# Gated linear attention with a mixture of experts: half of the values by POOL's queue, the output gate as a load of its own, and another order of SP's list of transfers

## The chip, the cores and the metric

The kernel runs on one core of a Trainium2 chip. The metric is the device time of one execution in microseconds (us); several executions of the same kernel are timed and their median is given. The core has five engines that follow lists of instructions of their own: TensorE (PE), VectorE (DVE), ScalarE (ACT), GpSimd (POOL) and SyncE (SP). SP does no arithmetic here, it issues transfers. POOL does arithmetic and issues transfers too, on a queue of its own. All transfers are carried out by the core's 16 DMA engines.

## The reference

Two stages follow each other. The first is a recurrent attention with gates, for 4 batches x 8 heads, 768 time steps and 40 values a head. The second takes its output as 3072 rows of 320 values, picks the best two of 8 experts for each row from noisy logits, and adds up the two experts' two-layer networks (320 to 1024 to 320).

```python
for t in range(S):
    m_new = max(f[t] + m, i[t])
    C = exp(f[t] + m - m_new) * C + exp(i[t] - m_new) * v[t] k[t]^T
    n = exp(f[t] + m - m_new) * n + exp(i[t] - m_new) * k[t]
    y[t] = sigmoid(o_gate[t]) * (C q[t]) / max(|n . q[t]|, 1)
x = y as (3072, 320)
logits = x @ w_gate + log1p(exp(x @ w_noise)) * noise
top2, weights = best two logits of a row, softmax over these two
out[row] += weight * (relu(x[row] @ w1[e]) @ w2[e])    for both experts e of the row
```

## The kernel before

**Attention.** The recurrence is computed in blocks of 64 time steps. A *unit* is one such block of two batches with all their heads, 128 rows of x; there are 24 units (`NU`), in two runs of 12 (`NCH`). The two batches of a unit are its two *halves*: half 0 sits in partitions 0 to 63, half 1 in partitions 64 to 127. For a unit u:

- `load_unit(u, what)` (L164) issues its loads on SP: q and k for the scores (tile `qk`, two transfers, L169), and the tile `vk`, two transfers of 64 rows x 968 values (L173 for half 0, L174 for half 1). One such row holds the 328 values with their ones, 320 of k, and 320 of the output gate. Each tile has four slots, so unit u uses slot u % 4.
- `e_part` (TensorE, L323, and ACT's exponential, L326) makes the decay weights `w` from the gates; `s_part` (L343, L346) the scores from `qk`; `k_part` (DVE, L354) weighs k; `p_part` (DVE, L360) multiplies scores and weights to `p`; `c_part` (TensorE L374, ACT L377) carries the state on into the next unit's slot of `vk`; `o_part` (TensorE, L383) makes the outputs from `vk` and `p`.
- `sig_part` (ACT, L332) turns the output gate (`SG`, a part of the `vk` tile) into its sigmoid in place, in three steps; `f_part` (DVE L388 to L394, POOL L395) divides and multiplies by it: the result `xr` is the unit's 128 rows of x.
- `keep_rows(u)` (L397) stores `xr` in DRAM: on POOL's queue for the first 12 units, on SP's afterwards. `t_part` (TensorE, L406) transposes `xr`, and from that the two gates of the experts, the choice of two, and the ranks of rows within their experts are computed, spread over the later steps.

**The main loop** (L821 on) runs over i with three units in hand: in turn i it computes the output of unit i, the scores of unit i + 2 and the weights of unit i + 2, and loads unit i + 3. Units 0 to 3 are loaded before and at the loop's start. What one turn puts into SP's list is, in this order: the stores of gate weights that are waiting in a list `sent` (L825; they write `wts`, the two weights of each row of earlier units, which POOL computes at L592), the loads of unit i + 3, the store of x of unit i − 1, in every second turn three small moves of attention gates (`gate_move`, L234 to L240: `le` and `re` out of `hl`; POOL issues them in turns below 13, SP later), and pieces of the first expert's W1 (L132), of constants or of noise. SP works through its list in order: an instruction whose inputs or whose slot aren't ready holds all that stand behind it. The same holds for POOL, whose list has, besides `xr`, the stores and the gate moves, a part of W1's split into two numbers (`w1l`, L142), `wts` and memsets.

**Experts.** From about 132 us on TensorE multiplies the gathered rows (`xg`, gathered by POOL at L779, rows transposed at L809) with each expert's W1 and W2, in two-number precision (L1003, L1032 to L1034). The outputs are scattered by POOL (L1055).

The order on TensorE, DVE and ACT is written out by hand by these calls, and `fill` and `SHARE` decide how much of the choice of experts goes into a turn.

Of the kernel before, what the change touches and what calls it, by code (L numbers as in the profile page):

```python
# [18 lines left out]
NE, F, DM = 8, 1024, 320  # L19
L = 64  # L20
TA = 4
NCH = S // L
NU = 2 * NCH
# [29 lines left out]
VW = 968  # L53
# [10 lines left out]
@with_exitstack  # L64
def build(ctx, tc, qk, vk, fi, noise, wgn, w1, w2, cst, ce, out):
    nc = tc.nc
    V, A, P, T, SP = nc.vector, nc.scalar, nc.gpsimd, nc.tensor, nc.sync
# [49 lines left out]
    SG = [t[:, 0, 648:VW] for t in VKS]  # L117
# [45 lines left out]

    def load_unit(u, what="kv"):  # L164
        pr, c = divmod(u, NCH)
        if "k" in what:
            r = 0
            for a, step, n in DIMS:
                SP.dma_start(QK[u % 4][a:128:step], qk[pr, c, r:r + n])  # L169
                r += n  # L170
        if "v" in what:
            flat = VKS[u % 4].rearrange("p x c -> p (x c)")
            SP.dma_start(flat[0:64, 0:VW], vk[pr, c, 0])  # L173
            SP.dma_start(flat[64:128, 648:648 + VW], vk[pr, c, 1])  # L174

# [24 lines left out]
    SP.dma_start(fit[:, :, 256:512], fi[:, :, 256:512])  # L200
    load_unit(0, "v")

# [68 lines left out]
    load_unit(1, "k")  # L271
    load_unit(1, "v")
    blank(2, P)
# [10 lines left out]
    for i in range(2, 4):  # L284
        keys(i)
    load_unit(2, "v")
    load_unit(3, "k")
# [109 lines left out]
    def keep_rows(u):  # L397
        (P if u < XV - 1 else SP).dma_start(XD[128 * u:128 * u + 128, 0:DM], XR[u])
# [274 lines left out]
    sent = []  # L673
# [45 lines left out]
    gate_move(2)  # L719
    load_unit(3, "v")  # L720
    SP.dma_start(fit[:, :, 512:], fi[:, :, 512:])
# [98 lines left out]
    i = 0  # L820
    while i < NU - LEAD:  # L821
        unit[0] = i
        spent[0] = 0.0
        while sent:
            SP.dma_start(*sent.pop())  # L825
        if 1 <= i and i + 3 < NU:
            load_unit(i + 3)
        if i:
            keep_rows(i - 1)
        if i % 2 == 0 and i and i // 2 + 2 < 2 * GB:  # L830
            gate_move(i // 2 + 2, (P, P) if i < XV else (SP, SP))
# [7 lines left out]
        if i == 5:  # L839
            SP.dma_start(nzt, noise)  # L840
        if not begun and done[0] >= E0U[0]:
            decode(0, E0S[1] // 128, 128 * E0U[0] > FIT)
            begun = 1
# [60 lines left out]
    u = NU - 2  # L904
# [19 lines left out]
    u = NU - 1  # L924
# [395 lines left out]
def layout(i):  # L1320
    import numpy as np
    z = lambda *s: np.zeros(s, np.float32)
    qk = z(2, NCH, 2, D, 2, H, L)
# [4 lines left out]
    qk = np.concatenate([qk[:, :, :, d].reshape(2, NCH, -1, 2, H, L) for d in (slice(0, DA), slice(DA, D))], 2)  # L1328
    vk = z(2, NCH, 2, L, VW)
    a = i["v"].reshape(2, 2, H, NCH, L, D).transpose(0, 3, 1, 4, 2, 5)  # L1330
    v = np.ones(a.shape[:-1] + (D + 1,), np.float32)
    v[..., :D] = a
    k, og = [i[n].reshape(2, 2, H, NCH, L, D).transpose(0, 3, 1, 4, 2, 5).reshape(2, NCH, 2, L, DM) for n in ("k", "o_gate")]
    for p in range(2):
        vk[:, :, p, :, 320 * p:320 * p + 328] = v.reshape(2, NCH, 2, L, 328)[:, :, p]
        vk[:, :, p, :, 320 * p + 328:320 * p + 648] = k[:, :, p]
        vk[:, :, p, :, 648 * (1 - p):648 * (1 - p) + 320] = og[:, :, p]
    fi = np.stack([i["f_gate"].reshape(2, 1, 16, S), i["i_gate"].reshape(2, 1, 16, S)], 3)
    fi = np.ascontiguousarray(np.broadcast_to(fi, (2, 2, 16, 2, S))).reshape(64, 2, S)
    nz = np.ascontiguousarray(i["moe_noise"].reshape(2, 2, NCH, L, NE).transpose(1, 3, 0, 2, 4)).reshape(128, NU, NE)  # L1340
# [5 lines left out]
    c, e = consts()  # L1346
    return dict(qk=qk, vk=vk, fi=fi, noise=nz, wgn=wgn, w1=i["moe_w1"], w2=i["moe_w2"], cst=c, ce=e)

# [19 lines left out]
```

## Time and profile before

| | us |
|---|---|
| median of 3 runs | 527.76 |
| lowest, highest | 525.27, 527.85 |
| the profiled execution | 528.23 |
| its span (first to last instruction) | 526.4 |
| TensorE busy | 504.1 |
| DVE, ACT, POOL busy | 343.1, 249.9, 215.7 |

The mean granted clock of TensorE is 0.993 of the full clock in the profiled execution.

A page of the profile has the busy time of each engine, a picture of the span in 40 slices, the DMA queues, a chain of work that ended last, and the costliest groups of instructions. Finer views answer questions: the instructions of one engine in order of time in a stretch (start, duration, engine, line, operation, tiles, count; in brackets the idle time just ahead of it and what ended this), the waits of SP's queue, the chain of waits in order of time, and a table of engines over stretches. Equal instructions in a row are merged in a line with their count, so the times of neighbouring lines of TensorE overlap. A line of the kernel is named L with its number. "SPq" is SP's list of transfers; its times are those of the issue, not of the transfer. Numbers of buffers are left out of names in these views.

### The profile page before, as it was taken

The page shows a single profiled execution, that of the slowest core. Times are in us where ns is not written, and L with a number is a line of the kernel's source. Part 1 is how long each engine was busy: PE and PEld are TensorE (multiplying, and loading weights), DVE is VectorE, ACT ScalarE, POOL GpSimd, SP SyncE. Part 2 cuts the span into 40 slices and gives each one's busy share as a digit, 9 for nine tenths or more (in the row PEclk, how much of TensorE's full clock was granted, in tenths as well). Part 3 has the DMA queues.
Part 4 walks back from the last instruction along what each step waited for, and adds up shares of the span by engine and source line. Part 5 has one row for each costly group of instructions (what it writes and reads, how often), then busy time and mean ns, then how long its engine had stood idle before and what let it go on. Part 6 is the DMA issues. An engine that isn't in the chain of part 4 may idle for free.

```text
span 526.4 us, 13193 instructions
## 1 busy us (share of the span) xinstructions
PE 504.1 (96%) x5052; PEld 473.3 (90%) x5053; DVE 343.1 (65%) x963; ACT 249.9 (47%) x607; POOL 215.7 (41%) x270
## 2 busy tenths in 40 slices
PE   9899998998999899999999999999999999999994
PEld 4778887987988788999999999999999999999994
DVE  8986979999887377763765485367447447645410
ACT  8877777888623145441543353154325415514300
POOL 6355455164012746145515623460553245042033
PEclk9998999999999999999999999999999999999998
DMA  5799797779767527069329515931762493272033
GB/s 155 191 258 246 212 228 199 191 217 252 262 197 243 96 40 207 17 124 256 84 55 269 103 37 105 265 91 37 213 141 63 97 263 86 55 175 25 2 36 44
DMA packets 49749, 76.79 MB, mean 146 GB/s; under 512 B 10425, under 2 KB 39616, under 8 KB 49680
## 3 DMA queue, kind: packets, MB, share of 16 engines
q1 hardware_dynamic: 38752, 57.18, 38.1%
q0 software_dynamic: 10928, 18.70, 18.8%
q8 instruction: 42, 0.69, 0.5%
q14 instruction: 27, 0.22, 0.2%
HBM read 52.27 MB, written 17.48 MB: 132 GB/s over the span
## 4 chain that ended last, share of the span: by engine, by line
PE 81%; DVE 8%; DMA 3%; issue 2%; SPq 2%; POOL 2%; ACT 1%; POOLq 0%; DVEq 0%
PE s L1003 24%; PE e L1003 11%; PE o L1032 5%; PE o L1033 5%; PE o L1034 5%; PE st L1033 5%; PE st L1032 5%; PE st L1034 5%; PE o L383 3%; PE s L346 3%; PE st L374 2%; PE e L323 2%; PE xt L426 2%; DMA qk<-qk_in 1%; DVE p L360 1%
## 5 line engine op out<-in xcount | busy, mean ns | idle before, releaser
L1055 POOL DMA_INDIRECT y_out<-y,tok x53 | 87.1, 1644 | 191.6 <-DVE y L1045 188.7
L1012 ACT ACTIVATE hh<-s 128x384 fp32r<-128x384 f32 (+3 forms) x91 | 42.8, 470 | 88.5 <-PE s L1003 82.0
L1003 PE MATMUL s<-xh,w1h 128*128 128x384 f32 (+5 forms) x273 | 76.8, 338 | 1.5 <-DVE xh L813 0.7
L779 POOL DMA_INDIRECT xg<-rows,tok x53 | 59.5, 1123 | 28.5 <-issue 14.2
L1015 DVE SCALAR_TENSOR_TENSOR hlo<-s,hh 128x384 fp32r<-128x384 f32 (+3 forms) x91 | 47.7, 525 | 27.1 <-ACT hh L1012 23.2
L1003 PE MATMUL s<-xh,w1l 128*128 128x384 f32 (+5 forms) x273 | 62.5, 336 | 0.7 <-DVE xh L813 0.7
L1033 PE MATMUL o<-w2l,hh 128*128 128x320 f32 x184 | 57.3, 312 | 0.0
L1032 PE MATMUL o<-w2h,hh 128*128 128x320 f32 x184 | 57.2, 311 | 0.0
L1034 PE MATMUL o<-w2h,hlo 128*128 128x320 f32 x184 | 56.6, 308 | 0.0
L1033 PE MATMUL st<-w2l,hh 128*128 128x320 f32 x176 | 54.9, 312 | 0.4 <-issue 0.4
L1032 PE MATMUL st<-w2h,hh 128*128 128x320 f32 x176 | 54.6, 310 | 0.1
L1034 PE MATMUL st<-w2h,hlo 128*128 128x320 f32 x176 | 54.1, 307 | 0.0
L1003 PEld LDWEIGHTS s<-xh,w1h 128*128 128x128 f32 x273 | 48.9, 188 | 3.5 <-ACT hh L1012 1.0
L1003 PEld LDWEIGHTS s<-xh,w1l 128*128 128x128 f32 x273 | 47.9, 188 | 2.2 <-DVE xh L813 0.9
L1003 PE MATMUL s<-xl,w1h 128*128 128x384 f32 (+5 forms) x182 | 46.4, 336 | 0.0
L1012 ACT ACTIVATE hh<-e 128x384 fp32r<-128x384 f32 (+3 forms) x45 | 21.3, 474 | 42.5 <-PE e L1003 39.8
L1045 DVE TENSOR_SCALAR y<-o,gw 128x320 f32<-128x320 f32 x23 | 12.6, 550 | 43.3 <-PE o L1034 43.3
L1045 DVE TENSOR_SCALAR y<-st,gw 128x320 f32<-128x320 f32 x22 | 12.1, 550 | 43.8 <-PE st L1034 43.8
L395 POOL TENSOR_TENSOR xr<-tm,vk 128x320 f32<-128x320 f32 x24 | 20.9, 872 | 46.6 <-ACT vk L332 13.6
L1003 PE MATMUL e<-xh,w1h 128*128 128x384 f32 (+5 forms) x135 | 38.6, 340 | 0.3 <-DVE ht L1023 0.3
L1032 PEld LDWEIGHTS o<-w2h,hh 128*128 128x128 f32 x184 | 34.6, 188 | 0.2 <-DVE y L1045 0.2
L1034 PEld LDWEIGHTS o<-w2h,hlo 128*128 128x128 f32 x184 | 34.7, 188 | 0.0
(234 smaller groups left out, 1243.8 us busy)
## 6 DMA issues: line engine op xcount, KB each, us to landing
vk<-vk_in SPq DMA_DIRECT2D x48, 242.0 KB
raw<-w_in SPq DMA_DIRECT2D x7, 1280.0 KB
raw<-w_in SPq DMA_DIRECT2D x7, 1024.0 KB
qk<-qk_in SPq DMA_DIRECT2D x24, 256.0 KB
raw<-w_in SPq DMA_DIRECT2D x19, 256.0 KB
y_out<-zrow SPq DMA_DIRECT2D x15, 320.0 KB
xt__2782<-xb SPq DMA_DIRECT2D x36, 72.0 KB
rows<-xr POOLq DMA_DIRECT2D x12, 160.0 KB
```

The source lines that it names most:

```text
L346: T.matmul(SQ[u][:, p][half[p], h, :], q[r, 1, h, :], q[r, 0, h, :], start=True, stop=True)
L383: T.matmul(OQ[u][half[p], h, :], PP[u][n, p, h, :], VK[u % 4][p][n, h * 41:h * 41 + 41], start=True, stop=True)
L395: P.tensor_mul(XR[u], tm.rearrange("p h d -> p (h d)"), SG[u % 4])
L779: P.indirect_dma_start(out=XG[0:rows_of(t), t], out_offset=None, in_=XD[0:n], in_offset=bass.IndirectOffsetOnAxis(ap=token(e, t), axis=0), ...
L1003: T.matmul(ps[:, 0:n], l, r, start=i == 0, stop=i == len(ops) - 1)
L1012: A.activation(hi, x, AF.Relu)
L1015: V.scalar_tensor_tensor(lo, x, 0.0, hi.bitcast(F32), op0=OP.max, op1=OP.subtract)
L1032: T.matmul(ps, HH[:, j, c], W2H[:, j], start=j == 0, stop=False)
L1033: T.matmul(ps, HH[:, j, c], W2L[:, j], start=False, stop=False)
L1034: T.matmul(ps, HLO[:, j, c], W2H[:, j], start=False, stop=j == 7)
L1045: V.tensor_scalar(y[0:n], ps[0:n], GW[e][0:n, t:t + 1], None, op0=OP.mult)
L1055: st = P.indirect_dma_start(out=out, out_offset=bass.IndirectOffsetOnAxis(ap=token(e, t), axis=0), in_=y[0:n], in_offset=None, compute_op= ...
```

## The change

The tile `vk` of a unit now comes in three transfers in place of two: 64 rows x 648 values (values and k, no gate) of half 0 on SP, the same of half 1 on POOL's queue, and the output gate of both halves as one transfer of 128 rows x 320 on SP, from an input `og` that the host lays out apart. So the input `vk` is 648 wide in place of 968. In a turn's part of SP's list the order becomes: loads of qk and of half 0, store of x, gate, gate moves, pieces of W1 or others, and the stores of gate weights last. The lines of the changed kernel are 2 higher than before up to the loop, and 4 higher behind it; the store of weights is L844. Lists of TensorE, DVE and ACT keep their order.

```diff
-    def load_unit(u, what="kv"):
+    def load_unit(u, what="kvg"):
...
         if "v" in what:
             flat = VKS[u % 4].rearrange("p x c -> p (x c)")
-            SP.dma_start(flat[0:64, 0:VW], vk[pr, c, 0])
-            SP.dma_start(flat[64:128, 648:648 + VW], vk[pr, c, 1])
+            for p in range(2):
+                (P if p else SP).dma_start(flat[64 * p:64 * p + 64, VW * p:VW * p + 648], vk[pr, c, p])
+        if "g" in what:
+            SP.dma_start(SG[u % 4], og[pr, c])
...
-        while sent:
-            SP.dma_start(*sent.pop())
         if 1 <= i and i + 3 < NU:
-            load_unit(i + 3)
+            load_unit(i + 3, "kv")
         if i:
             keep_rows(i - 1)
+        if 1 <= i and i + 3 < NU:
+            load_unit(i + 3, "g")
         if i % 2 == 0 and i and i // 2 + 2 < 2 * GB:
             gate_move(i // 2 + 2, (P, P) if i < XV else (SP, SP))
...
         if i == 5:
             SP.dma_start(nzt, noise)
+        while sent:
+            SP.dma_start(*sent.pop())
...
-    vk = z(2, NCH, 2, L, VW)
+    vk = z(2, NCH, 2, L, 648)
...
-        vk[:, :, p, :, 320 * p:320 * p + 328] = v.reshape(2, NCH, 2, L, 328)[:, :, p]
-        vk[:, :, p, :, 320 * p + 328:320 * p + 648] = k[:, :, p]
-        vk[:, :, p, :, 648 * (1 - p):648 * (1 - p) + 320] = og[:, :, p]
+        vk[:, :, p, :, 0:328] = v.reshape(2, NCH, 2, L, 328)[:, :, p]
+        vk[:, :, p, :, 328:648] = k[:, :, p]
```

At the start `load_unit(0, "v")`, `load_unit(1, "v")` and `load_unit(2, "v")` become the same calls with "vg", and so does that of unit 3.

SP's list where the loads of unit 16 stand (turn 13), before. The numbers behind the names are those of buffers: qk_105 and vk_109 are the slots of unit 16, raw_120 is a piece of W1 that belongs to turn 12; `rows<-xr` is a store of x, `rows<-wts` the store of gate weights.

```order
L132 DMA raw_120<-w_in 64x1024
L825 DMA rows<-wts 128x4x16
L169 DMA qk_105<-qk_in 64x1024
L169 DMA qk_105<-qk_in 16x1024
L173 DMA vk_109<-vk_in 64x968
L174 DMA vk_109<-vk_in 64x968
L398 DMA rows<-xr 128x320
L169 DMA qk_106<-qk_in 64x1024
```

The same place of SP's list with the change:

```order
L132 DMA raw_120<-w_in 64x1024
L169 DMA qk_105<-qk_in 64x1024
L169 DMA qk_105<-qk_in 16x1024
L174 DMA vk_109<-vk_in 64x648
L400 DMA rows<-xr 128x320
L176 DMA vk_109<-og_in 128x320
L844 DMA rows<-wts 128x4x16
L169 DMA qk_106<-qk_in 64x1024
```

The store of gate weights moved from ahead of unit 16's loads to behind the store of x and the gate's load; the load of half 1 is gone from SP's list.

POOL's list about turn 12, before: from `xr` of unit 11 to `xr` of unit 12 (slot vk_109 holds unit 12 there).

```order
L395 TENSOR_TENSOR xr<-tm,vk_112 128x320
L142 TENSOR_TENSOR w1l<-raw_120,w1h 128x512
L894 MEMSET xg 128x336
L398 DMA rows<-xr 128x320
L238 DMA le_99<-hl 32x2x64
L240 DMA re_97<-hl 1x16x128 x2
L592 TENSOR_TENSOR wts<-d_1515,wts 128x4
L395 TENSOR_TENSOR xr<-tm,vk_109 128x320
```

The same place of POOL's list with the change:

```order
L397 TENSOR_TENSOR xr<-tm,vk_112 128x320
L142 TENSOR_TENSOR w1l<-raw_120,w1h 128x512
L898 MEMSET xg 128x336
L174 DMA vk_112<-vk_in 64x648
L400 DMA rows<-xr 128x320
L240 DMA le_99<-hl 32x2x64
L242 DMA re_97<-hl 1x16x128 x2
L594 TENSOR_TENSOR wts<-d_1530,wts 128x4
L397 TENSOR_TENSOR xr<-tm,vk_109 128x320
```

The load of half 1 of unit 15 has come in ahead of the store of x, the gate moves, `wts` and the `xr` of unit 12.

SP's list at its end for attention, before: the loads of units 22 (qk_107, vk_111) and 23 (qk_108, vk_112).

```order
L169 DMA qk_107<-qk_in 64x1024
L169 DMA qk_107<-qk_in 16x1024
L173 DMA vk_111<-vk_in 64x968
L174 DMA vk_111<-vk_in 64x968
L398 DMA rows<-xr 128x320
L169 DMA qk_108<-qk_in 64x1024
L169 DMA qk_108<-qk_in 16x1024
L173 DMA vk_112<-vk_in 64x968
L174 DMA vk_112<-vk_in 64x968
L398 DMA rows<-xr 128x320
```

The same with the change:

```order
L169 DMA qk_107<-qk_in 64x1024
L169 DMA qk_107<-qk_in 16x1024
L174 DMA vk_111<-vk_in 64x648
L400 DMA rows<-xr 128x320
L176 DMA vk_111<-og_in 128x320
L169 DMA qk_108<-qk_in 64x1024
L169 DMA qk_108<-qk_in 16x1024
L174 DMA vk_112<-vk_in 64x648
L400 DMA rows<-xr 128x320
L176 DMA vk_112<-og_in 128x320
```

As many instructions stand ahead of qk of unit 23 as before, counted from qk of unit 22; one of them is the gate's load behind the store of x in place of the second half of `vk` ahead of it.

## Rows read from the trace of the kernel before

**Rows 1.** The page: the span, and TensorE's busy time, share of the span and instructions.

```profile
span 526.4 us, 13193 instructions
PE 504.1 (96%) x5052; PEld 473.3 (90%) x5053; DVE 343.1 (65%) x963; ACT 249.9 (47%) x607; POOL 215.7 (41%) x270
```

**Rows 2.** Table of three stretches: stretch, its length, busy time of each engine with its instructions, granted clock of TensorE, mean busy share of the 16 DMA engines, GB/s.

```profile
24.00:48.00 24.00, 21.66 (x502) 19.21 (x501) 19.23 (x43) 17.40 (x45) 12.28 (x20) 0.93 1.04 271
...
112.00:116.00 4.00, 3.45 (x65) 2.87 (x63) 4.00 (x23) 3.08 (x8) 2.88 (x3) 1.00 0.61 156
116.00:128.00 12.00, 10.42 (x268) 9.26 (x269) 11.59 (x28) 10.37 (x26) 5.97 (x7) 1.00 1.03 275
```

**Rows 3.** The chain of waits in order of time: start, us, what. "issue" is time in which the engine waited for nothing that the profile shows.

```profile
86.94 0.14 issue
...
118.26 7.16 DMA qk<-qk_in
```

**Rows 4.** TensorE's instructions at the end of the attention stage (start, us, engine, line, operation, in brackets the idle time before).

```profile
119.89 0.27 PE L346 MATMUL s<-qk 64*64 64x64 f32 x2 [0.48 <-DMA qk<-qk_in]
...
121.61 1.13 PE L383 MATMUL o<-vk,p 128*64 128x41 f32 x32
...
125.55 0.27 PE L346 MATMUL s<-qk 64*64 64x64 f32 x2 [0.59 <-DMA qk<-qk_in]
...
127.27 1.13 PE L383 MATMUL o<-vk,p 128*64 128x41 f32 x32
...
130.53 1.13 PE L383 MATMUL o<-vk,p 104*64 104x41 f32 x32
```

**Rows 5.** Waits of SP's list: who waited for whom, us in total, times, longest.

```profile
SPq L825 <- POOL wts L592: 6.3, 2, 4.1
```

**Rows 6.** SP's list in order of time about the loads of units 16 and 17, and the load of unit 23.

```profile
76.63 0.59 SPq L132 DMA_DIRECT2D raw<-w_in  x1
81.39 0.39 SPq L825 DMA_DIRECT2D rows<-wts  x1
81.84 1.32 SPq L169 DMA_DIRECT2D qk<-qk_in  x2
83.32 0.48 SPq L173 DMA_DIRECT2D vk<-vk_in  x1
83.89 0.54 SPq L174 DMA_DIRECT2D vk<-vk_in  x1
84.48 0.58 SPq L398 DMA_DIRECT2D rows<-xr  x1
85.11 1.16 SPq L169 DMA_DIRECT2D qk<-qk_in  x2
...
117.73 1.14 SPq L169 DMA_DIRECT2D qk<-qk_in  x2
```

**Rows 7.** TensorE's instructions about unit 13: the output part of unit 13, and the transposition of the `xr` of unit 12.

```profile
81.67 1.13 PE L383 MATMUL o<-vk,p 128*64 128x41 f32 x32
...
83.66 0.53 PE L406 MATMUL xt<-cs,xr 128*128 128x128 f32 x3
```

**Rows 8.** POOL's instructions about unit 12, in order of time.

```profile
76.88 1.87 POOL L142 TENSOR_TENSOR w1l<-raw,w1h 128x512 fp32r<-128x512 f32 x1 [1.44 <-ACT w1h L139]
...
79.01 0.57 POOL L398 DMA_DIRECT2D rows<-xr  x1
...
81.15 0.22 POOL L592 TENSOR_TENSOR wts<-d,wts 128x4 f32<-128x4 f32 x1
81.31 0.87 POOL L395 TENSOR_TENSOR xr<-tm,vk 128x320 f32<-128x320 f32 x1
```

**Rows 9.** DVE's instructions in the same stretch: `p` of units 21, 22 and 23.

```profile
120.11 1.22 DVE L360 TENSOR_TENSOR p<-s,w 128x1024 f32<-128x1024 f32 x1
...
124.97 1.22 DVE L360 TENSOR_TENSOR p<-s,w 128x1024 f32<-128x1024 f32 x1
...
128.31 1.21 DVE L360 TENSOR_TENSOR p<-s,w 128x1024 f32<-128x1024 f32 x1
```

**Rows 10.** Groups of POOL's instructions in 20 to 122 us by line: count, busy us, mean ns of one, idle time before.

```profile
L398 POOL DMA_DIRECT2D rows<-xr x12 | 7.2, 598 | 1.8 <-POOL xr L395 0.6 <-DVE xg L222 0.3 <-DMA qk<-qk_in 0.3
```

**Rows 11.** The page's list of transfers: the loads of `vk`, count and KB of one.

```profile
vk<-vk_in SPq DMA_DIRECT2D x48, 242.0 KB
```

**Rows 12.** TensorE's instructions in 34 to 48 us, two places with a stop.

```profile
36.47 0.31 PE L383 MATMUL o<-vk,p 128*64 128x41 f32 x2 [1.14 <-issue]
...
44.09 0.27 PE L346 MATMUL s<-qk 64*64 64x64 f32 x2 [1.10 <-issue]
```

**Rows 13.** Table of stretches, columns as in rows 2: the stretch behind the second stop.

```profile
44.00:48.00 4.00, 3.91 (x92) 3.79 (x92) 1.51 (x4) 1.79 (x7) 2.24 (x5) 0.57 1.05 293
```

**Rows 14.** The chain of waits in 38 to 49 us: the first scores and the first gate product of two units that follow each other.

```profile
38.39 0.20 PE s L346 x2
...
41.18 0.43 PE e L323
...
44.09 0.27 PE s L346 x2
...
48.45 0.42 PE e L323
```

**Rows 15.** The page's list of DMA queues (packets, MB, share of 16 engines): one of the two that carry instructions.

```profile
q8 instruction: 42, 0.69, 0.5%
```

More of the change, by code (lines that the diff above doesn't have):

```diff
@@ L64, in build @@
 @with_exitstack
-def build(ctx, tc, qk, vk, fi, noise, wgn, w1, w2, cst, ce, out):
+def build(ctx, tc, qk, vk, og, fi, noise, wgn, w1, w2, cst, ce, out):
     nc = tc.nc
@@ L200, in build @@
     SP.dma_start(fit[:, :, 256:512], fi[:, :, 256:512])
-    load_unit(0, "v")
+    load_unit(0, "vg")
     def run(steps):
@@ L271, in build @@
     load_unit(1, "k")
-    load_unit(1, "v")
+    load_unit(1, "vg")
     blank(2, P)
@@ L285, in build @@
         keys(i)
-    load_unit(2, "v")
+    load_unit(2, "vg")
     load_unit(3, "k")
@@ L719, in build @@
     gate_move(2)
-    load_unit(3, "v")
+    load_unit(3, "vg")
     SP.dma_start(fit[:, :, 512:], fi[:, :, 512:])
@@ L1346, in layout @@
     c, e = consts()
-    return dict(qk=qk, vk=vk, fi=fi, noise=nz, wgn=wgn, w1=i["moe_w1"], w2=i["moe_w2"], cst=c, ce=e)
+    return dict(qk=qk, vk=vk, og=og.reshape(2, NCH, 128, DM), fi=fi, noise=nz, wgn=wgn, w1=i["moe_w1"], w2=i["moe_w2"], cst=c, ce=e)
 OUT_ROWS = NTOK + BLK
```

## The prediction

> **What bounds the kernel now.** I read the page first: TensorE is busy 504.1 of 526.4 us [rows 1]. From 132 us on its chain has no gap that a load of this change could close, so what can move lies in the attention stage, 15 to 132 us. In the table of stretches the DMA engines are full in 24–48 and in 116–128 us (share 1.04 and 1.03) and slack between, 0.61 at 112–116 [rows 2]. Third, the chain of waits: its one long stretch that is no engine's work is a load of q and k, 7.16 us from 118.26 [rows 3]. Fourth, TensorE's list of instructions about it: it waits for a load of q,k twice, 0.48 us before 119.89 (scores of unit 22) and 0.59 us before 125.55 (scores of unit 23) [rows 4]. These two are all that TensorE waits for on vk, the gates or qk; 1.07 us is what a better list of loads could give at most, if nothing else is late behind them.
>
> Why are those loads late? SP's waits show the store of gate weights (L825) held for POOL's wts, 6.3 us in two times, the longest 4.1 [rows 5]. SP's own list shows the place: the piece of W1 is issued by 77.22 (76.63 + 0.59), the store goes out only at 81.39, and behind it in the list stand qk and vk of unit 16 (81.84) and, after the store of x at 84.48, qk of unit 17 at 85.11 [rows 6]. From there SP doesn't catch up: six units later, qk of unit 23 goes out at 117.73, (117.73 − 85.11) / 6 = 5.44 us a unit [rows 6], while TensorE needs (121.61 − 81.67) / 8 = 4.99 us a unit between the output parts of units 13 and 21 [rows 4, 7]. So SP loses 0.45 us a unit to the consumer and has used up its lead by unit 22.
>
> **The change part by part.** *Gate weights last.* In unit 13's list the two qk loads and SP's half of vk now stand ahead of that store, and go out at about 77.2 instead of 81.8. But the store of x of unit 12 now stands ahead of the gate's load and of the store of weights, and it needs xr of unit 12, which POOL ends at 82.18 (81.31 + 0.87) [rows 8]. So SP's hold is not removed, only what stands behind it: store of x, gate, weights, then qk of unit 17. The store takes 0.63 (84.48 to 85.11), the gate's load the same, the weights 0.45 (81.39 to 81.84) [rows 6]. If xr were as punctual as before, qk of unit 17 goes out at 82.3 + 1.7 = 84.0, 1.1 us earlier than 85.11. But POOL has one more issue ahead of xr(12) (next part, 0.58), and everything from its 76.88 to its 81.31 is packed, so 84.5 and a lead of 0.55 is what I take. From there SP's list has the same number of issues a unit (qk twice, one vk, one gate in place of the other vk, x), so the lead stays to unit 23, within some 0.05 us a unit: 64-row loads take 0.48 and 0.54, a 128-row transfer 0.58 [rows 6].
>
> *What an earlier qk gives.* For unit 22 most of the 0.48 us is worth nothing: the next output part (121.61) needs p, which DVE ends at 120.11 + 1.22 = 121.33 [rows 9], and 0.14 us pass from DVE's end to TensorE's start [rows 3], so 121.47 is the floor: gain 121.61 − 121.47 = 0.14. For unit 23, p ends at 124.97 + 1.22 = 126.19 and the output part began at 127.27 [rows 4, 9]; the whole 0.59 is to be had. Together 0.73. What is late next is p of unit 23, done at 128.31 + 1.21 = 129.52, with 0.14 behind it 129.66; the output part at 130.53 moved up by 0.73 stands at 129.80, so it still holds [rows 4, 9].
>
> *The second half of vk by POOL's queue.* 24 more issues on POOL. POOL's own issues of a 128-row store take a mean of 598 ns [rows 10], SP's of a 64-row half of vk 480 and 540 [rows 6], so 0.48 to 0.60 each; 0.58 taken, 14 us over the stage. POOL isn't on the path as such; only its lateness counts. The densest place is unit 12: from w1l at 76.88 through the store at 79.01 and the gate moves to wts at 81.15 and xr at 81.31 it has no gap [rows 8]; the issue goes ahead of them all, xr(12) ends 82.76 instead of 82.18, and TensorE transposes it at 83.66 [rows 7]. Slack 1.48, used 0.58: nothing on the path, except the 0.55 us of SP's lead already taken off above. If the cover were gone (no slack at all), that place would cost 0.58 once.
>
> The Trainium skill speaks against this at that very place: by "SBUF — State Buffer", section "SBUF: two separate sides", while VectorE runs an instruction that uses both ports GpSimd can't write descriptors for its DMAs. No run here shows such a hold; POOL's twelve stores in this stage have a mean of 598 ns [rows 10], while DVE is busy 19.23 of 24 us in 24–48 [rows 2]. By the rule the issue at unit 12 could grow by one DVE instruction (1.22 us), 1.80 against a slack of 1.48, and the sum would lose 0.3 us and SP's lead as well; by the trace it is 0.
>
> *The queue beside SP's.* A transfer on POOL's queue no longer stands behind SP's loads. Before, vk of unit 23 was issued behind qk of unit 23; now its second half may be served beside it. The half is 64 x 648 x 4 bytes = 166 kB, and at the 275 GB/s of that stretch [rows 2] that is 0.60 us for all engines. Bounds for qk(23): 0.60 later (all of it served first) or 0 (behind it). So its landing moves between −1.1 and +0.05 us against before. Bytes are the same: two loads of 242 KB a unit [rows 11] become 162 + 162 + 160. I take the middle, half a us earlier: 0.14 of unit 22 and 0.46 of the 0.59 of unit 23, **−0.6 us**.
>
> *The gate apart in 128 rows.* It is loaded in the turn three units ahead, and the first step of its sigmoid on ACT comes two turns later: 2 x 4.99 = 10.0 us for a landing of 7.16 at the longest shown [rows 3], so 2.8 us are left. 0. *The start.* POOL issues four vk halves in its first blocks, two issues less stand on SP there, two gates more: 0 within 0.3 us either way.
>
> Sum: 528.23 (profiled execution: 526.4 span and 1.8 around it) − 0.6 = 527.6. That execution stands 0.47 above the median of the runs, 527.76; on the median it is **527.2 us**.
>
> **The rivals.**
> *Nothing moves.* POOL's half pushes qk(23) back by the full 0.60 and xr(12) is late by 0.58, which eats the 1.1. For: both are in the bounds above. Against: all bad ends have to meet. Time 527.8.
>
> *Faster, by TensorE's own stops.* TensorE stops without anything that the profile shows as releaser: 1.14 us before 36.47 and 1.10 before 44.09 [rows 12]. Behind the second the granted clock is 0.57 in 44–48 [rows 13], about the lower level of 1.2 GHz for most of it. From scores to the next gate product it took 48.45 − 44.09 = 4.36 there and 41.18 − 38.39 = 2.79 a unit earlier [rows 14]: the slow clock cost 1.57, with the stop 2.67. Code comes by the same 16 engines (queue q8 moved 0.69 MB [rows 15]), in a stretch with a share of 1.04; the change puts other transfers there. If the stop falls away or shrinks, the clock stays up: 527.2 − 2.67 = 524.5. For: the stops lie where the engines are fullest. Against: the bytes are the same, and nothing in the change asks for less.
>
> *Slower, the same mechanism with the other sign.* POOL's loads now run beside SP's list in 24–48, so code arrives later, and a unit that ran clean (38–41 us) gets a stop of 1.1 us and the clock drop: +2.67, 529.8, or 530.4 if the 0.6 isn't had. The point from which it decides is a stop after which the clock falls, as before 44.09; a stop after which the clock stays up, as a unit ahead at 36.47 (the unit of 2.79 us behind it ran unhindered), costs its own length alone, 1.1 us, and stays inside the forecast's half per cent.
>
> *The change doesn't do what it says*: SP stays held about as long as before (to 82.3 or 82.9, before 81.39). That is part of the forecast.
>
> **How the numbers follow.** Forecast 0.46 (own range 526.6 to 527.8, all gain or none); nothing moves 0.16 (527.8); faster by a stop 0.21 (524.5, spread 523.5 to 525.5); slower by a stop 0.17 (529.8, spread 528.5 to 531). The range reaches past the centres of both side cases, 524.1 to 530.0; outside it lie a third of each, 0.13 in all. A measurement of this kernel tells about 0.5%, 2.6 us, from no change: faster means under 525.1, slower over 530.4. Faster: 0.8 of the third case and 0.06 for the runs' own spread (one of three was 525.27), 0.23. Slower: half of the fourth and 0.02, 0.11. Same 0.66.
>
> **What would show it.** Right: SP issues qk of unit 16 near 77.3 and then waits for xr(12) at its store of x; qk of unit 23 is issued 0.5 to 1.1 us earlier; TensorE's wait before the scores of unit 23 shrinks to under 0.2; the chain of waits has no long load at 118. POOL: 24 more issues of 0.5 to 0.6 us and xr(12) 0.6 later, not waited for. Wrong: POOL's issues are far over 0.6 us, so xr is waited for by TensorE; or the stops and the clock in 24–48 us differ, and the difference in time is theirs; or a wait for vk or the gate shows on DVE or ACT in front of TensorE.

## The result, and the profile after

Over 20 runs each the changed kernel has a median of 530.79 us and the kernel before one of 528.18 us; the ratio is 1.0051 with a 95% interval of 1.0030 to 1.0071. So it is slower by half a per cent, 2.6 us, where 0.6 us less was forecast; 530.79 lies above the range (524.1 to 530.0). The profiled execution of the changed kernel took 529.92 us, 1.69 more than that of before. Ratios, and the medians of the experiments, leave disturbed executions out; the two medians above hold all 20.

The page of the changed kernel, span and busy times, answering [rows 1]:

```profile
span 528.1 us, 13192 instructions
PE 507.6 (96%) x5052; PEld 476.8 (90%) x5053; DVE 344.3 (65%) x963; ACT 250.2 (47%) x607; POOL 227.6 (43%) x294
```

TensorE is busy 3.5 us longer for the same 5052 instructions: its work ran slower for a while. The table of stretches (columns as in [rows 2]; 16 to 24 us is added) shows where:

```profile
16.00:24.00 8.00, 7.99 (x144) 6.76 (x144) 5.94 (x12) 4.85 (x11) 1.98 (x4) 0.50 0.77 200
24.00:48.00 24.00, 23.18 (x564) 20.65 (x561) 20.39 (x47) 18.81 (x47) 12.80 (x22) 0.96 0.87 258
112.00:116.00 4.00, 3.45 (x74) 2.87 (x75) 4.00 (x22) 3.00 (x7) 3.04 (x3) 1.00 0.73 225
116.00:128.00 12.00, 10.83 (x271) 9.51 (x266) 11.59 (x26) 10.56 (x25) 7.83 (x9) 1.00 0.76 235
```

and the kernel before in the added stretch:

```profile
16.00:24.00 8.00, 6.81 (x173) 5.74 (x173) 7.01 (x15) 6.63 (x16) 1.91 (x3) 1.00 0.70 172
```

In 16 to 24 us the granted clock is 0.50, the lower of its two levels (1.2 GHz), against 1.00 before. In 24 to 48 and 116 to 128 us the DMA engines are no longer full (0.87 and 0.76, before 1.04 and 1.03). Just ahead of the slow stretch TensorE stands still; the changed kernel's TensorE in order of time:

```profile
15.84 1.11 PE L376 MATMUL st<-vk,kd 64*40 64x41 f32 x26 [1.83 <-DVE kd L356]
...
23.50 1.92 PE L385 MATMUL o<-vk,p 128*64 128x41 f32 x32
```

It waits 1.83 us for `kd` of unit 0, and behind it, at the lower clock, the output part of unit 1 takes 1.92 us (1.10 in the kernel before). The same stop of the kernel before was 0.40 us:

```profile
15.02 0.81 PE L374 MATMUL st<-vk,kd 64*40 64x41 f32 x32 [0.40 <-DVE kd L354]
```

The product starts 0.82 us later (15.84 against 15.02); the stop is longer by more than that because TensorE arrives 0.61 us earlier. `kd` is late because of VectorE's chain ahead of it, and that is late because of one load. VectorE at the start of the changed kernel, its second scan over the attention gates and the first `kd`:

```profile
7.37 0.56 DVE L212 TENSOR_TENSOR_SCAN xg<-raw,xg 64x128 f32<-64x128 f32 x1 [1.25 <-DMA raw<-fi_in]
...
14.97 0.81 DVE L356 TENSOR_TENSOR kd<-vk,w 128x640 f32<-128x640 f32 x1
```

and in the kernel before:

```profile
6.45 0.67 DVE L210 TENSOR_TENSOR_SCAN xg<-raw,xg 64x128 f32<-64x128 f32 x1 [0.37 <-DMA raw<-fi_in]
...
14.16 0.81 DVE L354 TENSOR_TENSOR kd<-vk,w 128x640 f32<-128x640 f32 x1
```

The scan waits 1.25 us for its part of the gate inputs in place of 0.37, and from there on all is 0.8 to 0.9 us late. SP issued that load at 4.15 us before and 4.14 us after; what is new beside it stands in POOL's list:

```profile
1.63 1.34 POOL L174 DMA_DIRECT2D vk<-vk_in  x2
...
7.20 0.45 POOL L263 COPY vk<-cs 40x320 f32<-40x320 f32 x1 [2.44 <-DMA cs<-cst_in]
```

POOL issues the second halves of units 0 and 1 at 1.63 us, long before anyone needs them, and 2 x 162 KB run in the 16 DMA engines together with the gate inputs, the first qk and the constants (POOL's first copy from `cs` starts at 7.20, before at 6.39). The Trainium skill ("DMA: Bandwidth & Descriptors", section "Queues, rings and completion order") says that each DMA engine serves the queues it has work for in turn. The trace fits this, in that a load that SP issued at the same time as before came later with POOL's loads beside it; the turns themselves no view shows. In the kernel before these halves stood in SP's list behind the gate inputs, at 6.05 and 10.71 us.

The second half of the change did what it was to do. SP's list about unit 16 and at its end, answering [rows 6]:

```profile
76.79 1.22 SPq L169 DMA_DIRECT2D qk<-qk_in  x2
78.12 0.53 SPq L174 DMA_DIRECT2D vk<-vk_in  x1
81.90 0.35 SPq L400 DMA_DIRECT2D rows<-xr  x1
82.34 0.48 SPq L176 DMA_DIRECT2D vk<-og_in  x1
82.92 0.41 SPq L844 DMA_DIRECT2D rows<-wts  x1
83.38 1.23 SPq L169 DMA_DIRECT2D qk<-qk_in  x2
...
115.72 1.13 SPq L169 DMA_DIRECT2D qk<-qk_in  x2
```

qk of unit 16 goes out 5.1 us earlier, SP then waits for xr of unit 12 as foreseen, qk of unit 17 is 1.7 and qk of unit 23 2.0 us earlier. Both of TensorE's waits for qk at the end are gone; its list there, answering [rows 4]:

```profile
119.14 0.27 PE L348 MATMUL s<-qk 64*64 64x64 f32 x2
...
124.71 0.27 PE L348 MATMUL s<-qk 64*64 64x64 f32 x2
...
126.99 1.13 PE L385 MATMUL o<-vk,p 104*64 104x41 f32 x32 [0.36 <-DVE p L362]
...
130.96 1.13 PE L385 MATMUL o<-vk,p 104*64 104x41 f32 x32 [0.76 <-PE xt L408]
```

The scores of unit 23 begin at 124.71, 0.84 earlier than before. But the output part of unit 23 comes at 130.96, 0.43 *later*. It waits for VectorE, whose list has no gap here:

```profile
124.11 1.01 DVE L392 SCALAR_TENSOR_TENSOR dn<-dn 128x8 f32<-128x8 f32 x1
...
128.74 1.21 DVE L362 TENSOR_TENSOR p<-s,w 128x1024 f32<-128x1024 f32 x1
...
130.37 0.49 DVE L396 SCALAR_TENSOR_TENSOR tm<-dn,o 128x320 f32<-128x320 f32 x1
```

All units' outputs go into one buffer (`name="o"`), so that output part can't begin before VectorE has read the output of unit 22 (`tm`, to 130.86, 0.10 us ahead of it). In the kernel before the same `tm` ended 0.10 us ahead of it too:

```profile
129.94 0.49 DVE L394 SCALAR_TENSOR_TENSOR tm<-dn,o 128x320 f32<-128x320 f32 x1
```

129.94 + 0.49 = 130.43, and [rows 4] has the output part at 130.53. So TensorE's earlier scores gave nothing at the end of the stage. What made it a loss in this execution is VectorE's `dn` at 124.11, which took 1.01 us (0.17 before). It ends at 125.12, where a piece of W1's split on POOL ends too (123.80 + 1.29 = 125.09):

```profile
123.80 1.29 POOL L142 TENSOR_TENSOR w1l<-raw,w1h 64x512 fp32r<-64x512 f32 x1 [2.74 <-ACT vk L334]
```

In the kernel before this piece starts at 125.83, behind that `dn`, and lies beside four instructions of VectorE that follow. Beside which ones POOL's pieces fall differs from trace to trace. From the start of `p` of unit 21 to the end of `tm` of unit 22 VectorE takes 10.94 us here and 10.32 before, but over all traces in which it waits no longer than 0.3 us there, it takes 9.2 to 10.9 with the change's order and 9.6 to 10.7 in the kernel before and its variants. So a lasting cost of the change at this place isn't shown.

Followed instruction by instruction (TensorE's order is the same in both), the changed kernel stands 3.6 us behind at 25.5 us, 0.4 behind at 67, 0.3 ahead at 111, 0.4 behind at 134, and 1.0 behind from 186 us on; the rest lies in the tail. The start's loss was nearly made up in this pair of traces, since the one of before lost 2.67 us to the stop and fall of the clock at 44 us and 1.14 to the stop at 36 [rows 12 to 14], which the other didn't have. What this means for the median had to be tried.

### The profile page after: what moved, and what is told of

The parts are those of the page before. It is cut to its first block, busy times and chain, and to the rows that moved or that the text cites. A ratio compares the mean times of both kernels' runs of the same rounds, so it can differ in the third digit from the quotient of the medians.

```text
span 528.1 us, 13192 instructions
## 1 busy us (share of the span) xinstructions
PE 507.6 (96%) x5052; PEld 476.8 (90%) x5053; DVE 344.3 (65%) x963; ACT 250.2 (47%) x607; POOL 227.6 (43%) x294
## 4 chain that ended last, share of the span: by engine, by line
PE 75%; DVE 14%; ACT 4%; issue 3%; POOL 2%; DMA 2%; SPq 0%; POOLq 0%; DVEq 0%
PE s L1007 23%; PE e L1007 11%; PE o L1037 5%; PE o L1036 5%; PE o L1038 5%; PE st L1037 5%; PE st L1036 5%; PE st L1038 5%; PE o L385 3%; DVE p L362 3%; PE s L348 2%; DVE ob L639 2%; PE e L325 2%; PE st L376 1%; DVE kd L356 1%
## 5 line engine op out<-in xcount | busy, mean ns | idle before, releaser
L385 PE MATMUL o<-vk,p 104*64 104x41 f32 (+2 forms) x768 | 30.0, 237 | 5.2 <-DVE p L362 2.5
```

The source lines that it names most:

```text
L385: T.matmul(OQ[u][half[p], h, :], PP[u][n, p, h, :], VK[u % 4][p][n, h * 41:h * 41 + 41], start=True, stop=True)
```

## The experiments

Two theories went in. **S**: POOL's two early loads delay the gate inputs; the stop and the fall of the clock at 16 us are the loss (S2 in the second group: the same, with chance stops of TensorE in 15 to 50 us on top of it in every kernel). **L**: the loss lies in the loop, in POOL's other 22 issues or in the order of SP's list. Kernels of one group ran on one chip; the kernel before ran in each group, and its median differs between them (528.18 in the first measurement, then 529.75, 530.23, 528.94 and 527.41 in groups 1 to 4), so only members of a group are compared. The expectations of group 1 name times that start from 528.18; they are read as distances to before. "Clock up to" gives the highest mean granted clock of any execution of a kernel.

**1. The early loads issued later** (group 1).

```diff
             for p in range(2):
-                (P if p else SP).dma_start(flat[64 * p:64 * p + 64, VW * p:VW * p + 648], vk[pr, c, p])
+                if p == 0 or u > 1:
+                    (P if p else SP).dma_start(flat[64 * p:64 * p + 64, VW * p:VW * p + 648], vk[pr, c, p])
...
     for i in range(2):
         keys(i)
+        P.dma_start(VKS[i].rearrange("p x c -> p (x c)")[64:128, VW:VW + 648], vk[0, i, 1])
```

> The changed kernel, with POOL's loads of half 1 of units 0 and 1 issued behind its blocks keys(0) and keys(1), near 7 to 10 us, in place of 1.6 and 2.4 us. Theory S (the start): these two early loads stand beside the gate inputs in the 16 DMA engines, VectorE's second scan waits 1.25 us for its input in place of 0.37, kd of unit 0 is 0.8 us late, TensorE stops 1.83 us at 15.8 and its clock is at the lower level from 16 to 24 us; that is the loss. Then here the scan's wait is back at 0.4, no half clock in 16 to 24, and the time is 527 to 528.5, that of before or less. Theory L (the loop): POOL's other 22 issues or the list's order cost it, the start is made up by 48 us as in the one trace at hand; then the time stays at 530 to 531 though the start is mended.

Measured: median 528.66, before 529.75, ratio 0.9962 (0.9923 to 1.0000); clock up to 0.994. The scan's wait is back at 0.40 us:

```profile
6.56 0.71 DVE L213 TENSOR_TENSOR_SCAN xg<-raw,xg 64x128 f32<-64x128 f32 x1 [0.40 <-DMA raw<-fi_in]
```

TensorE's first product with `kd` runs at 14.11 without a stop. That is 0.91 us earlier than in the kernel before (15.02), though the scan starts no earlier than there. The edit has shortened something else, an instruction of VectorE behind the scan (a CAST to `hl`) that elsewhere runs beside POOL's clearing of a `qk` slot. VectorE and POOL in the kernel before, then in kernel 1:

```profile
8.94 1.38 DVE L227 CAST hl<-xg 64x256 fp32r<-64x256 f32 x1
...
9.22 0.95 POOL L188 MEMSET qk<- 128x1024 f32 x1
```
```profile
8.90 0.43 DVE L230 CAST hl<-xg 64x256 fp32r<-64x256 f32 x1
...
10.21 0.97 POOL L191 MEMSET qk<- 128x1024 f32 x1
```

Before, both end within 0.15 us of each other (10.32 and 10.17). In kernel 1 POOL's two issues stand ahead of the MEMSET, which comes after the CAST. In the ten traces without these moved issues, that of the changed kernel among them, the MEMSET starts 0.28 or 0.29 us behind the CAST and the CAST takes 1.37 or 1.38 us; in the four with them (kernels 1, 7, 11 and 12) it takes 0.28 to 0.43. So VectorE has about 1 us in these four that it has neither in before nor in the changed kernel; TensorE's first product with `kd` starts at 14.11 to 14.86 in them, 0.2 to 0.9 us ahead of the first trace of before. A comparison with them holds this as well as the late load.

Now TensorE is ahead of the loads:

```profile
18.66 0.37 PE L350 MATMUL s<-qk 64*64 64x64 f32 x2 [1.80 <-DMA qk<-qk_in]
```

The clock in 16 to 24 us is 0.79, with this stop in it. S is right about the late load; what the start gives is partly taken by the next load.

**2. The early loads alone, in the kernel before** (group 1).

```diff
-            SP.dma_start(flat[64:128, 648:648 + VW], vk[pr, c, 1])
+            (P if u < 2 else SP).dma_start(flat[64:128, 648:648 + VW], vk[pr, c, 1])
```

> The kernel before, with one thing of the change alone: half 1 (64x968) of units 0 and 1 by POOL's queue, issued at 1.6 and 2.4 us as in the changed kernel. Theory S: the whole loss is here, 530 to 531.5, with the scan's wait above 1 us and the half clock in 16 to 24 us. Theory L: 527.5 to 528.5, whatever the start shows.

Measured: median 530.66, before 529.75, ratio 0.9999 (0.9961 to 1.0038). Of its trace VectorE's second scan, TensorE's first product with `kd`, and the stretch behind it, each from the view that was shown above:

```profile
8.93 0.49 DVE L210 TENSOR_TENSOR_SCAN xg<-raw,xg 64x128 f32<-64x128 f32 x1 [2.65 <-DMA raw<-fi_in]
```
```profile
17.34 1.00 PE L374 MATMUL st<-vk,kd 64*40 64x41 f32 x26 [1.84 <-DVE kd L354]
```
```profile
16.00:24.00 8.00, 6.54 (x106) 5.30 (x108) 6.60 (x13) 3.80 (x9) 0.95 (x4) 0.60 0.63 157
```

All of the start's signs come with these two loads alone, and TensorE stands 3.7 us behind at 25.5 us. Against the kernel before the time is a miss for S: 0.9 us by the medians, none by the ratio, whose interval leaves room for 2 us either way. Against kernel 1 of the same group it is 2.0 us slower, and part of that is the shorter CAST of kernel 1 (0.9 us at TensorE's first product with `kd`).

**3. Gate weights last, nothing else** (group 1).

```diff
-        while sent:
-            SP.dma_start(*sent.pop())
         if 1 <= i and i + 3 < NU:
...
             SP.dma_start(nzt, noise)
+        while sent:
+            SP.dma_start(*sent.pop())
```

> The kernel before, with the stores of gate weights last in a turn's part of SP's list and nothing else. Prediction's sum: the qk of unit 16 goes out 4 us earlier, the two waits of TensorE for qk at 119.9 and 125.6 go, and the time falls by 0.6. Rival (VectorE is full in 116 to 132 us, 11.6 of 12 us, and the output part of unit 23 waits for VectorE's tm of unit 22): the waits go and the time doesn't move, within 0.3. Theory L for the order: 529.5 or more.

Measured: 529.75, the median of before in this group; ratio 0.9969 (0.9933 to 1.0005). TensorE has no wait for qk after 118 us, the store of weights goes out behind the store of x (86.52 behind 85.43). By the interval the order costs no more than 0.3 us; whether it brings anything isn't told. Start as before: stop of 0.38 us, clock 1.00 in 16 to 24.

**4. Half 1 by POOL from unit 4 on, nothing else** (group 1).

```diff
-            SP.dma_start(flat[64:128, 648:648 + VW], vk[pr, c, 1])
+            (P if u > 3 else SP).dma_start(flat[64:128, 648:648 + VW], vk[pr, c, 1])
```

> The kernel before, with half 1 (64x968, gate included) by POOL's queue from unit 4 on only; start and order as before. Theory S: 527.5 to 528.5, since POOL's issues in the loop are hidden; SP has one issue less a unit (3 in place of 4 loads), so qk of unit 23 goes out some us earlier and TensorE's waits for qk go. Theory L: 529.5 to 531, with DVE or TensorE later in the loop than before.

Measured: 530.72, ratio 1.0035 (0.9997 to 1.0074): inconclusive, its interval holds 1; by the medians it is 1.0 above before. That is nearer to L than to S, and a cost of POOL's issues in the loop isn't excluded. qk of unit 23 goes out at 115.03, and TensorE doesn't wait for qk. Its trace lost 5 us at 28.56, where TensorE waited 2.06 us for a load of router weights and the clock fell (0.80 and 0.77 in 24 to 40 us).

By now four traces without the early loads had stops at four different places between 18 and 50 us. So the second group repeated both kernels.

**5. Before, again** (group 2; no edit).

> The kernel before, once more, as one of the kernels of this group. It gives a second trace of before and the spread of its time and clock where the others are measured. Theory S2 (chance and the start): stops of TensorE in 15 to 50 us differ from one execution of a kernel to the next (loads and code that come late while the 16 DMA engines are full), each with a fall of the clock behind it; the time is set by their sum, and the offset at 60 us stays to the end. So this trace has other stops than the first one of before, its time spreads over 525 to 534, and the highest granted clock of its runs is 0.995 or more (an execution with hardly a fall). Theory L: the same stops at the same places as in the first trace.

Measured: 529.57 (530.23 in the runs beside the other kernels of the group), clock up to 0.997. The waits for qk at the end, on which my gain rested, aren't in this trace: TensorE waits for no load after 110 us. Stops at other sizes: 0.82 at the first `kd`, no fall of the clock there; 0.65 at 36.51, and 1.45 at 44.48, this time with the clock at 1.00 throughout 24 to 48 us. S2's picture, not L's.

**6. The changed kernel, again** (group 2; no edit).

> The changed kernel, once more. Theory S2: in all of its runs VectorE's second scan waits for the gate inputs about 1.2 us, TensorE stops at about 16 us and its clock falls there; so no run has a granted clock over 0.992, this trace shows 0.5 to 0.6 in 16 to 24 us, and its median lies 2 to 3 us above that of before in this group. Theory L: the fall at 16 us is chance, this trace may lack it, and the clock reaches 0.995 in some run.

Measured: 530.82, ratio 1.0015 (0.9982 to 1.0048); no clock above 0.990. The same three rows of its trace:

```profile
8.55 0.48 DVE L212 TENSOR_TENSOR_SCAN xg<-raw,xg 64x128 f32<-64x128 f32 x1 [2.45 <-DMA raw<-fi_in]
```
```profile
16.95 0.81 PE L376 MATMUL st<-vk,kd 64*40 64x41 f32 x32 [2.09 <-DVE kd L356]
```
```profile
16.00:24.00 8.00, 5.54 (x104) 4.32 (x106) 6.94 (x13) 4.27 (x10) 2.71 (x7) 0.70 0.81 200
```

The scan waits 2.45 us, TensorE stops 2.09 us, the clock falls, 4.5 us behind the first trace of before at 25.5 us. TensorE then waits another 1.15 us for qk at 21.29. The fall at the start is no chance. But the distance to before is 0.6 us by the medians of this group and 0.8 by the ratio, not 2 to 3.

**7. Early loads later, and the gate of unit 1 behind qk of unit 2** (group 2).

```diff
-    load_unit(1, "vg")
+    load_unit(1, "v")
...
     load_unit(2, "k")
+    load_unit(1, "g")
```

> The changed kernel with POOL's first two loads behind keys(0) and keys(1), as in the first mended kernel, and the gate's load of unit 1 behind the qk loads of unit 2 on SP: there TensorE waited 1.80 us for qk of unit 2 at 18.66, after an issue of that load that took 1.59 us. Theory S2: that wait goes or falls below 0.8, no fall of the clock in 16 to 24 us; median 1 to 3 us below that of the changed kernel, and the lowest of this group, 527 to 528.5. Theory L: 530 to 531.

(The edit of kernel 1 is in it.) Measured: 529.06, ratio 0.9999 (0.9970 to 1.0028), 1.8 us under the changed kernel in its group; the short CAST (0.28 us) is in it. At 25.5 us it is 0.7 us *ahead* of before; then it runs into the next load:

```profile
30.81 0.37 PE L351 MATMUL s<-qk 64*64 64x64 f32 x2 [3.34 <-DMA qk<-qk_in]
```

It is 4.4 us behind at 31.5 and level at 50.

**8. All loads on SP** (group 2).

```diff
-                (P if p else SP).dma_start(flat[64 * p:64 * p + 64, VW * p:VW * p + 648], vk[pr, c, p])
+                SP.dma_start(flat[64 * p:64 * p + 64, VW * p:VW * p + 648], vk[pr, c, p])
...
-    load_unit(0, "vg")
+    load_unit(0, "v")
...
-    load_unit(1, "vg")
+    load_unit(1, "v")
...
     load_unit(2, "k")
+    load_unit(0, "g")
+    load_unit(1, "g")
```

> The changed kernel with all its loads on SP: half 1 behind half 0 of each unit, the gates of units 0 and 1 behind qk of unit 2; list order of the changed kernel otherwise. It tells what POOL's queue is worth in the loop. SP has 0.55 us more to issue a unit: about 6.0 us a unit where TensorE takes 5.0, so it falls behind by 1 us a unit from unit 16 on, TensorE waits for qk of units 20 to 23, together 3 to 5 us, and the time is 531 to 533. If SP had slack after all, it is that of before, and POOL's queue is worth nothing.

Measured: 529.88, ratio 1.0005 (0.9968 to 1.0043); the number is better than expected, the mechanism is there. TensorE waits at the end:

```profile
117.01 0.47 PE L327 MATMUL e<-re,le 98*128 98x512 f32 x1 [1.14 <-DMA re<-hl]
...
120.65 0.27 PE L350 MATMUL s<-qk 64*64 64x64 f32 x2 [1.91 <-DMA qk<-qk_in]
```

and goes from 1.8 us ahead of before at 117 to 2.3 behind at 123. So in the change's order SP's list has no room for another load of a unit at the end of the stage, and POOL's queue is what carries it in the changed kernel.

**Why the start's loss isn't the whole difference.** Kernels 1, 3, 4, 7 and 8, which start on time or early, wait 1.3 to 3.3 us for a load between 18 and 35 us. (The kernel before doesn't in its two traces, 0.47 us at most; it has the stops at 36 and 44 us.) In the traces that start late such a wait is shorter: none in the changed kernel and in kernel 2, 1.15 us in kernel 6 and, later, 0.97 in kernel 10. At 52 us the first three of these stand 0.4 to 1.6 us behind the first trace of before, in place of 3.6 to 4.5. (Kernel 2 stops for 3.31 us at 42.44 without a releaser, so the pattern isn't clean.) That asks whether loads set the pace in 24 to 48 us. Kernels 9 to 11 leave out 160 KB a unit in units 4 to 9: the output gates there aren't loaded, or only 8 of 320 columns of them (group 3). Theory **R**: what is lost at the start is regained as far as the loads are late anyway.

**9. Before, fewer bytes** (group 3).

```diff
+            n = 320 if 4 <= u <= 9 else 0
-            SP.dma_start(flat[0:64, 0:VW], vk[pr, c, 0])
-            SP.dma_start(flat[64:128, 648:648 + VW], vk[pr, c, 1])
+            SP.dma_start(flat[0:64, 0:VW - n], vk[pr, c, 0, :, 0:VW - n])
+            SP.dma_start(flat[64:128, 648 + n:648 + VW], vk[pr, c, 1, :, n:VW])
```

> The kernel before with 160 KB less a unit in units 4 to 9: their output gates aren't loaded (old values in the slot are used), the number of transfers is the same. Theory R (regained): in 24 to 48 us the loads set the pace, the DMA engines run at a share of 1.03 to 1.05 with 6 to 7.5 us from issue to landing, and TensorE runs into late loads of qk and into stops behind them. With 0.96 MB less (3.5 us at 271 GB/s) these stops go: share in 24 to 48 under 0.95, TensorE's time lost there falls, its work stands 1.5 to 3 us earlier at 62 us than in the traces of before, and the median falls by 1 to 3 us. Rival (stops of TensorE have nothing to do with loads): the same stops, the median within 0.7 of before.

Measured: 526.56, before 528.94, ratio 0.9948 (0.9916 to 0.9980). Its TensorE stands 3.7 us earlier at 62 us than in the first trace of before, with

```profile
24.00:48.00 24.00, 22.73 (x552) 20.37 (x552) 20.39 (x49) 19.76 (x52) 13.07 (x23) 1.00 0.98 259
```

The stops at 36 and 44 are down to one of 0.55, with a wait of 0.65 for qk at 28.25; the share of 0.98 is above the 0.95 that was expected. (This one execution lost its 3.7 us again between 116 and 132 us, to a stop of 2.82 us without a releaser and a clock of 0.79.) By the median R holds.

**10. The changed kernel, fewer bytes** (group 3).

```diff
+            n = 8 if 4 <= u <= 9 else DM
-            SP.dma_start(SG[u % 4], og[pr, c])
+            SP.dma_start(SG[u % 4][:, 0:n], og[pr, c, :, 0:n])
```

> The changed kernel with 8 of 320 columns of the gate loaded in units 4 to 9, same number of transfers. Theory R: the changed kernel is 3.6 to 4.5 us late at 25 us, and gets part of it back by 50 us because loads, not TensorE, set the pace there. With the loads relieved nothing is given back: it stays 3 to 4 us behind the kernel before with the same relief, so 527.5 to 530, and no run has a clock over 0.992. Rival: 0 to 1 us behind it.

Measured: 529.16, no clock above 0.990. 2.6 us behind kernel 9: with the loads relieved a good part of the loss stays, somewhat less than the 3 to 4 expected. The two differ by the whole change, start and loop. By the traces it stands 3.2 us behind kernel 9's at 111 us (0.6 and 3.8 ahead of the first trace of before).

**11. Kernel 7, fewer bytes** (group 3; the edit of kernel 10).

> The same relief with the start mended (POOL's first two loads behind keys(0) and keys(1), gate of unit 1 behind qk of unit 2). Theory R: as fast as the kernel before with the relief or up to 1 us faster, 3 to 4 us below the changed kernel with the relief; clock up to 0.995 or more. Rival (the loss is POOL's other issues or the list's order): as slow as the changed kernel with the relief.

Measured: 527.65, clock up to 0.997, 1.5 us under kernel 10 and 1.1 over kernel 9, so between the theories' numbers; its trace still has a wait of 2.20 us for qk at 29.57. Against L alone: with POOL's other issues and the new order it isn't as slow as kernel 10. The short CAST is in it.

**12. Kernel 1, again** (group 4).

> The changed kernel with POOL's first two loads behind keys(0) and keys(1), once more, since it was the lowest against before in its group (528.66 against 531.83) with an interval that touched 1. If the start is the loss and POOL's queue in the loop costs nothing, it is again not slower than before: its median 0 to 3 us below, its highest clock 0.993 or more, no fall of the clock behind the first product of kd at 14 to 16 us. If the lower median was chance, it is within 0.5 us of before or above.

Measured: 526.09, before 527.41, ratio 0.9971 (0.9931 to 1.0011); clock up to 0.998. There is no fall of the clock at the start; in this trace it falls later (0.50 in 32 to 40 us, behind a wait of 2.81 us for qk at 30.70). Averaged with kernel 1's first ratio: (0.9962 + 0.9971) / 2 = 0.9967, half width 0.0039 / √2 = 0.0028, so 0.994 to 0.9995. That would be a little faster than the kernel before, but the first of the two ratios was picked because it was the lowest, the second alone holds 1, and kernel 3 (0.9969) isn't told apart. Both traces also have the short CAST, 0.9 and 0.2 us at TensorE's first product, so that the change's loop has no part in the loss doesn't follow.

**All runs together.** The granted clock of an execution tells the two starts apart better than its time. Of the four kernels with POOL's two early loads (the changed kernel twice, 2 and 10) none of 56 runs has a mean clock over 0.992. Of the other nine, 38 of 108 have; of the kernel before in the four groups, 33 of 115 (one execution of 1225.73 us left aside). That fits a fall of the clock at the start in every one of the 56.

## Why the prediction was wrong

The step that failed is the start: "POOL issues four vk halves in its first blocks ... 0 within 0.3 us either way". I counted SP's issues and took POOL's for free, without asking what stands in the DMA engines at 2 to 7 us and who waits for it; my rows show nothing of the first 20 us. The term is a late load (0.9 to 2.3 us more wait at VectorE's scan in the four traces), a stop of TensorE of 1.83 to 2.12 us in place of 0.38 to 1.17, and a low clock behind it (0.50 to 0.70 in 16 to 24 us): together TensorE is 3.6 to 4.5 us late at 25 us. That the two loads do this is shown by kernels 1, 2 and 6.

What it costs at the end is less, and how much of the 2.6 us is the start's isn't shown. The whole change costs 2.6 us in the first measurement and with the loads relieved (kernels 9 and 10), 0.6 to 0.8 in group 2; the two loads alone cost 0.9 by the medians and nothing by the ratio (kernel 2). That part is regained, because a kernel that starts on time meets late loads in 24 to 48 us, fits kernels 7, 9 and 10. Why before lost less to them in the first measurement stays open. Whether the loop has a share stays open as well: kernel 4's interval leaves room for one, and kernels 1 and 12, with all of the loop in them and not slower than before, have the short CAST for it.

*SP's list.* Right in its order, with more gain than forecast: SP held at the store of x for xr of unit 12 (to 81.90; I said 82.3 or 82.9), qk of units 17 and 23 earlier by 1.7 and 2.0 (I took 0.55, as POOL's w1l ran 1.28 us in place of 1.87), both waits for qk gone.

*What that gives.* −0.6 forecast, nothing shown. The step "the output part at 130.53 moved up by 0.73 stands at 129.80, so it still holds" named the wrong floor: not p of unit 23 (129.66) but `tm` of unit 22, 130.43 + 0.10. VectorE is busy 11.59 of 12 us in 116 to 128 [rows 2], and I read that row for its DMA share only. In this trace the long `dn` made a loss of it. Besides, the waits for qk themselves come and go (kernel 5).

*POOL's issues.* Right as to their own time. Its 20 loads in 20 to 122 us took a mean of 551 ns, and xr of unit 12 wasn't waited for:

```profile
L174 POOL DMA_DIRECT2D vk<-vk_in x20 | 11.0, 551 | 0.0
```
```profile
78.20 0.54 POOL L174 DMA_DIRECT2D vk<-vk_in  x1
...
81.01 0.86 POOL L397 TENSOR_TENSOR xr<-tm,vk 128x320 f32<-128x320 f32 x1
```

The rule of the Trainium skill that I weighed ("SBUF — State Buffer", section "SBUF: two separate sides"), by which VectorE can hold back the descriptors of POOL's transfers, shows in none of these 20 loads: they took 0.53 to 0.60 us each, the issue at unit 12 0.54.

*The rivals.* "Slower by a stop", 0.17, came nearest: a stop and a fall of the clock, +2.67 worked out from another place. But I put it into 24 to 48 us and made it chance; it was the start's, in all four traces with the early loads. The stops in 24 to 48 that I counted on as given are themselves what changes from run to run.

## What to carry to other kernels

A load given to a second queue leaves the order of the first: it starts as early as that engine's list lets it (here at 1.63 us in place of 6.05 and 10.71), and then runs beside loads that are urgent. Before moving one, look at what lies in the DMA engines at the moment when it will now be issued, first of all in the opening microseconds, and put it behind something that the engine does anyway, as kernels 1 and 12 did. Look also at which instruction of VectorE the moved work of POOL will now run beside: here a CAST took 1.38 us in place of 0.28 to 0.43. Where a mended version comes out faster, find out first whether the mending moved something else. Take a gain at a wait only after following the next engine's list to its next gap: where VectorE has none, TensorE's earlier start is worth nothing (here scores 0.84 us earlier and an output part 0.43 later).

## What the runs showed that I had not expected

- The same kernel loses its time at different places from run to run: before had stops of 1.14 and 1.10 us at 36 and 44 us in one trace, 0.65 and 1.45 in another. Behind the 1.10 the clock fell (0.57 in 44 to 48), behind the 1.45 it stayed at 1.00.
- A start that is 3.6 us late can be nearly level at 67 us, when the kernel beside it stops in 24 to 48 us, where the DMA engines are full (share 1.04 in both traces of before). 160 KB less in each of six units are worth 2.4 us to the kernel before (526.56 against 528.94).
- Behind a stop of 1.80 us for qk at 18.66 in kernel 1 the clock fell, as it did behind the stop for `kd` (0.79 in 16 to 24 us).
- An instruction of VectorE that overlaps one of POOL's can last until that one ends: the CAST at 8.94 in ten traces, `dn` at the end of the stage in six (0.70 to 1.28 us in place of 0.14 to 0.17), where the two ends lie 0.01 to 0.03 us apart.
